# One-core delta-rule attention with two expert layers: two weight blocks loaded at a time from the first on, and eight stores of K Kᵀ moved from GpSimd's queue to SyncE's, behind 19 blocks

## The chip, the cores and the metric

One core of a Trainium2 chip runs the whole program. The time is device microseconds of that core, from launch to end; the number that is predicted is the median of repeated runs.

## What is computed

For each of 4 x 8 heads a state of 48 x 48 is carried over 768 tokens, and its 384 output features go through two expert layers. Cut to what matters:

```python
k_n = k / (norm(k) + 1e-6)
for t in range(S):
    y[:, :, t] = einsum('bhd,bhde->bhe', q[:, :, t], state)
    v_old = einsum('bhde,bhd->bhe', state, kt)
    state = state + bt * einsum('bhd,bhe->bhde', kt, vt - v_old)
x = y as (3072 tokens, 384)
h = max(x @ w_in, 0);  x = (h * h) @ w_out            # 384 -> 2048 -> 384
h = max(x @ w1, x @ w2, x @ w3);  out = h @ w_out2     # 384 -> 768 -> 384
```

## The kernel before

**Tiling.** The tokens are cut into 12 chunks of 64 (`c`), each chunk into two halves `p` of 16 heads. Inside a chunk the recurrence is solved in closed form: K Kᵀ of the chunk is turned into a triangular matrix whose inverse is built on DVE in blocks of 32 (`solve32`, lines 747 to 766). Chunks 0 and 1 are solved in a prologue, in blocks of 16 that PE joins afterwards (`join_z`, `join_w`, lines 952 to 971). Chunks 2 and 3 are solved later, from a K Kᵀ that is computed in the prologue too (`kk_matmul` with `second`, lines 939 to 949), copied by ACT into SBUF, stored to DRAM (`kk_d` the K Kᵀ part, `p_d` the Q Kᵀ part, eight stores of 256 KB) and read back in another layout by `start32` (line 315).

**Weights.** All weights are 64-bit floats in DRAM. A block of w_in (128 columns) or a row block of w_out is 384 KB; `fetch` (line 90) loads it on SyncE's queue, `turn` (line 116) makes two float32r parts of it. For each block ACT takes the sign away (line 107, for the first 12 blocks also line 112, else DVE's line 120), DVE joins the words (line 124), ACT rounds to the high part (line 128) and DVE subtracts to get the low part (line 132). There are 32 blocks: 0 to 11 are w_in into tiles `rawp`, then w_out and w_in take turns in seven buffers that are used in a ring (`raw` four, `big` three). So 19 blocks have a place of their own, and block 19 and on wait until a buffer is free.

**How many are under way.** Lines 97 to 99 give each of the first 19 blocks a wait: a block among the first 12 waits for the landing of the block ahead of it (`few = 1`), a later one for the landing of the second ahead (`few = 2`):

```python
few = 1 if len(raws) <= NP else 2
if few < len(raws) <= NP + NR + len(spare):
    tc.add_manual_dep(raws[-1], raws[-1 - few].name, ... reason="landed")
```

**Order.** The order on each engine is written in the program and pinned (`pin`, line 261). In `attention(0)` (line 1007) each step of chunk 0's attention is followed by the words of one or two blocks, so 12 blocks stand between the steps on ACT and DVE. After that `moe_a(0)` (line 581) is PE's main stream, with the remaining blocks (`weights`, line 775), the second join and chunk 1's attention between its steps; in the same way each later `moe_a(c)` carries the attention of chunk c + 1. From line 1066 on the second expert layer runs.

**Memory.** The prologue's tiles live in a pool `pkp` (`ks_more`, `kct`, `ksr`, `rawp`), which is closed at line 1016. The pools `gp` (`gh`, `gl`) and `moe` (`wout0` to `wout3`) take its place, so the first write of these waits until the old tiles are no longer read, by stores too.

**Queues.** SyncE issues keys and weight blocks in program order, and an instruction that waits holds up those behind it. GpSimd's queue issues the values and keys of attention (`load_att`, line 372), before also the eight stores (lines 946 and 948).

Of the kernel before, what the change touches and what calls it, by code (L numbers as in the profile page):

```python
# [36 lines left out]
U2 = 2 * Q  # L37


def delta_moe(ctx, tc, kc, ab, kt, vt, beta, beta32, beta16, kq, w_in, w_out, w1, w2, w3, w_out2, out):  # L40
    nc = tc.nc
    vec, act, pool = nc.vector, nc.scalar, nc.gpsimd
# [24 lines left out]
    kk_d = [dram.tile([2, C, 2, B * Q, C], F32, name=f"kk{g}", tag=f"kk{g}") for g in range(NC // 2)]  # L67
# [10 lines left out]
    NR, NP = 4, 12  # L78
# [11 lines left out]
    def fetch(src, shape, dma):  # L90
        raw = raw_tile(shape)
        names = "k n" if len(shape) == 2 else "n"
        flat = "k (n t)" if len(shape) == 2 else "(n t)"
        raws.append(dma.dma_start(raw.rearrange(f"p {names} t -> p {flat}"), src).ins)
        for i in raw_after:
            behind(raws[-1], i)
        few = 1 if len(raws) <= NP else 2
        if few < len(raws) <= NP + NR + len(spare):
            tc.add_manual_dep(raws[-1], raws[-1 - few].name, mybir.DependencyInfo(mybir.DependencyClass.Sync, mybir.DependencyReason.DATA), reason="landed")
        return raw  # L100

    def convert(src, hi, lo, shape, lo_eng, dma):
        turn(fetch(src, shape, dma), hi, lo, lo_eng)
# [60 lines left out]
    def two(d, c, p):  # L164

        return d[:, c, 2 * p:2 * p + 2]
# [9 lines left out]
    def kk_matmul(c, p, ps_, swap=1):  # L176

        k = kcs.pop((c, p))
        pk, pq = (ps_[0].tile([128, U2, C], F32, name=n, tag=ps_[1]) for n in ("pk", "pq"))
        for u in range(U2):  # L180
            for i, ps in enumerate((pk, pq)):
                for t in range(2):
                    r = slice(64 * t, 64 * t + D)
                    o = 64 * (t ^ i * swap)
                    pe.matmul(ps[o:o + 64, u], k[r, u, 0], k[r, u, i], start=True, stop=True)  # L185
        return pk, pq

    def kk_store(c, p, kk, dma=nc.sync):
        dma.dma_start(kk_d[c // 2].rearrange("t j c u i -> (t j) c u i")[:, c % 2, U2 * p:U2 * p + U2], kk)
# [71 lines left out]
    def pin():  # L261
        todo = []
        for i in reversed(nc.cur_bb.bb.instructions):
            if i.name == seen[0]:
                break
            todo.append(i)
        for i in reversed(todo):
            seen[0] = i.name
            if i.engine in pinned and i.name not in loose:
                if pinned[i.engine]:  # L270
                    behind(i, pinned[i.engine])
                pinned[i.engine] = i

    def behind(ins, before):

        tc.add_manual_dep(ins, before.name, mybir.DependencyInfo(mybir.DependencyClass.NoSync, mybir.DependencyReason.DATA), reason="order")
# [26 lines left out]
    def start32(g, dmas=(nc.sync, nc.sync)):  # L303
        cs = HALVED[g]
        u = 64 * len(cs)
        M = M32[0:u]
        a = early.tile([128, 32], F32, name="a32", tag="a32")[0:u]
        bt = early.tile([128, 32], F32, name="b32", tag="b32")[0:u]
        if g:
            dmas[0].dma_start(bt, beta_d[g].rearrange("x c u j -> (x c u) j"))  # L310
        else:
            halves[:] = [bt]
        for h, t, o in quarters if g else ():
            hs = slice(32 * h, 32 * h + 32)
            dmas[t].dma_start(M[o:o + 32], kk_d[g][t, hs, :, :, hs].rearrange("j c u i -> (c u) j i"))
        def ready():
            return prep(M, 32, u, bt, a, early, alone=not g, flip=g < 2)

        def norm(nm):
            pv = transposed(nm, 32, u).rearrange("j (s t c u) -> j c s t u", s=2, t=2, u=16)  # L320
            for t in range(2):
                for s in range(2):
                    o = 64 * t + 32 * s
                    i = act.activation(out=normT[o:o + 32, cs[0]:cs[0] + len(cs)], in_=pv[:, :, s, t], func=AF.Copy, scale=0.5)
            return i.ins
        return M, a, ready, norm
# [45 lines left out]
    def load_att(c, p):  # L372
        us = slice(U2 * p, U2 * p + U2)
        def load(to, src):
            pool.dma_start(to, src)
        kq_ = None
        if c:
            kq_ = att.tile([R2, U2, 2, C], F32, name="kq", tag="kq")
            i = pool.dma_start(kq_, two(kc, c, p).rearrange("p b q t s -> p (b q) t s"))
            for j in kq_after:  # L380
                behind(i.ins, j)
        v = att.tile([128, U2, D], F32, name="v", tag="v")
        load(v, two(vt, c, p).rearrange("p b q d -> p (b q) d"))
        pt_ = att.tile([128, U2, C], F32, name="p", tag="p")
        if c:
            pool.dma_start(pt_, p_d[c][:, us])
        kt_ = ktp[p]
        load(kt_[:, 0:U2 * D], two(kt, c, p).rearrange("p b q d -> p (b q d)"))
        tiles[c, p] = [kq_, v, xb[:, us], pt_, kt_, None, None, None, None]
# [336 lines left out]
    if True:  # L726
# [68 lines left out]
        for h in range(2):  # L795
            for n, (c, p) in enumerate(todo):
                i = (nc.sync, act)[p].dma_start(kcts[n][:, :, h], two(kc, c, p)[:, :, :, h].rearrange("p b q s -> p (b q) s"))
        M, a, _, norm = start32(0)
        bt = halves[0]
        for c in range(2):  # L800
# [6 lines left out]
        for n, dma in ((0, nc.sync), (1, act)):  # L807
            c, p = second[n]
            dma.dma_start(second_keys[n], two(kc, c, p).rearrange("p b q t s -> p (b q) t s"))
        wcols = lambda f: slice(128 * f, 128 * (f + 1))  # L810

        ins = lambda *fs: [(f, True) for f in fs]
# [95 lines left out]
        for n in range(2, 4):  # L908
            c, p = second[n]
# [20 lines left out]
            vec.tensor_tensor(out=of_, in0=of_, in1=tv, op=ALU.add)  # L930
        vec.memset(diagonal(M, 32), 1.0)
        vec.tensor_tensor(out=Mb, in0=Mb, in1=by_block(a, 2), op=ALU.mult)
        vec.transpose(out=turned_x.rearrange("p n i -> p i n"), in_=M)
        dt, zt = (wa.tile([128, KD, TB], F32R, name=n, tag=n, bufs=2).bitcast(F32).rearrange("p k t -> p (k t)")[:, 0:512].rearrange("p (n i) -> p n i", i=16) for n in ("xh", "xl"))
        last_turn = vec.transpose(out=dt.rearrange("p n i -> p i n"), in_=M[:, :, 0:16].rearrange("p j i -> p i j")).ins
        solved.append(last_turn)
        pin()

        second_ks = [(kss[2][:, 0], kss[3][:, 0]), (ks_more[:, 0], ks_more[:, 1]), (kss[0][:, 1], kss[2][:, 1]), (kss[3][:, 1], kss[0][:, 0])]
        for n in range(4):  # L940
            c, p = second[n]
            kcs[c, p] = second_keys[n]
            for i, (k, pk) in enumerate(zip(second_ks[n], kk_matmul(c, p, (p1, at)[n % 2], 0))):
                act.copy(k, pk)
                if i:
                    pool.dma_start(p_d[c][:, U2 * p:U2 * p + U2], k)
                else:
                    kk_store(c, p, k, pool)
            pin()
        joins = {}  # L950

        def join_z(c):
# [18 lines left out]
            return vec.tensor_sub(out=to, in0=to, in1=joins[c]).ins  # L971

        join_z(0)
        sign_next(1)
        joined = join_w(0)
        pin()
        pinned.clear()
# [196 lines left out]
```

## Time and profile before

| what | us |
|---|---|
| median of 3 runs | 942.15 (940.6 to 942.8) |
| profiled execution, its own time | 945.85 |
| its span in the trace | 944.1 |
| outside the span | 1.75 |
| mean granted clock of TensorE | 0.956 |

The rows further down are of the profiled execution. In a timeline row the first number is the start in us from the span's start, the second the time taken, then engine, line, operation, tiles; in brackets stands how long the engine had been idle and what ended that. "issue" there means that nothing in the profile ended the wait. A `q` behind an engine's name (SPq) is its queue, where DMAs are issued.

### The profile page before, as it was taken

The page shows a single profiled execution, that of the slowest core. Times are in us where ns is not written, and L with a number is a line of the kernel's source. Part 1 is how long each engine was busy: PE and PEld are TensorE (multiplying, and loading weights), DVE is VectorE, ACT ScalarE, POOL GpSimd, SP SyncE. Part 2 cuts the span into 40 slices and gives each one's busy share as a digit, 9 for nine tenths or more (in the row PEclk, how much of TensorE's full clock was granted, in tenths as well). Part 3 has the DMA queues.
Part 4 walks back from the last instruction along what each step waited for, and adds up shares of the span by engine and source line. Part 5 has one row for each costly group of instructions (what it writes and reads, how often), then busy time and mean ns, then how long its engine had stood idle before and what let it go on. Part 6 is the DMA issues. An engine that isn't in the chain of part 4 may idle for free.

```text
span 944.1 us, 27438 instructions
## 1 busy us (share of the span) xinstructions
PE 890.2 (94%) x11958; PEld 863.9 (92%) x11958; DVE 469.3 (50%) x1044; ACT 389.0 (41%) x824; POOL 141.4 (15%) x238
## 2 busy tenths in 40 slices
PE   7563899899999999999999999999999999999998
PEld 7553898799899999999999999999999999999998
DVE  5445778449726852784378354456332323323221
ACT  5454754335344534453444466565221222212211
POOL 6310210032222123112401320002000000000000
PEclk8765889799999999999999999999999999999999
DMA  9756723381475167326521743235201101000000
GB/s 239 225 163 198 216 88 92 98 182 41 113 219 123 64 143 184 99 64 178 135 73 63 169 140 87 65 104 142 60 19 41 34 26 34 18 26 9 17 17 34
DMA packets 113527, 95.43 MB, mean 101 GB/s; under 512 B 69880, under 2 KB 95240, under 8 KB 113408
## 3 DMA queue, kind: packets, MB, share of 16 engines
q1 hardware_dynamic: 93824, 52.84, 21.5%
q0 software_dynamic: 12352, 34.75, 13.1%
q10 hardware_dynamic: 7232, 6.10, 2.1%
q8 instruction: 94, 1.54, 0.7%
q14 instruction: 25, 0.20, 0.1%
HBM read 70.45 MB, written 22.77 MB: 99 GB/s over the span
## 4 chain that ended last, share of the span: by engine, by line
PE 79%; DMA 9%; DVE 7%; ACT 3%; issue 1%; DVEq 0%; SPq 0%
PE p L1082 24%; PE px L613 19%; PE p L593 19%; PE po L1099 8%; DMA rawp<-in_moe_w_in_dram 7%; DMA raw<-in_moe_w_out_dram 2%; PE pY L537 2%; PE pk L185 1%; PE pU L483 1%; DVE gl L602 1%; DVE buf L293 1%; PE pW L437 1%; DVE buf L294 1%; PE pA L464 1%; PE pq L185 1%
## 5 line engine op out<-in xcount | busy, mean ns | idle before, releaser
L1082 PE MATMUL p<-x_h,w 128*128 128x384 f32 x864 | 220.0, 336 | 0.0
L613 PE MATMUL px<-wout,gh 128*128 128x384 f32 x768 | 202.3, 344 | 0.0
L593 PE MATMUL p<-xh,win_h 128*128 128x256 f32 x576 | 171.8, 298 | 1.6 <-DVE gl L602 0.9
L593 PE MATMUL p<-xl,win_h 128*128 128x256 f32 x576 | 165.8, 288 | 0.3 <-DVE xl L559 0.3
L593 PE MATMUL p<-xh,win_l 128*128 128x256 f32 x576 | 165.9, 288 | 0.0
L1082 PEld LDWEIGHTS p<-x_h,w 128*128 128x128 f32 x864 | 156.2, 188 | 0.0
L1082 PE MATMUL p<-x_l,w 128*128 128x384 f32 x432 | 145.2, 336 | 0.0
L602 DVE TENSOR_TENSOR gl<-p,gh 128x512 fp32r<-128x512 f32 x96 | 66.3, 691 | 145.5 <-ACT gh L601 142.0
L613 PEld LDWEIGHTS px<-wout,gh 128*128 128x128 f32 x768 | 137.5, 192 | 1.2
L613 PE MATMUL px<-wout,gl 128*128 128x384 f32 x384 | 130.5, 340 | 0.0
L599 ACT ACTIVATE p<-p 128x512 f32<-128x512 f32 x96 | 55.9, 582 | 172.1 <-PE p L593 172.1
L593 PEld LDWEIGHTS p<-xh,win_h 128*128 128x128 f32 x576 | 112.6, 196 | 5.5 <-DVE gl L602 1.5
L593 PEld LDWEIGHTS p<-xl,win_h 128*128 128x128 f32 x576 | 113.1, 196 | 0.6 <-DVE xl L559 0.5
L593 PEld LDWEIGHTS p<-xh,win_l 128*128 128x128 f32 x576 | 113.0, 196 | 0.1
L1088 DVE TENSOR_TENSOR mx<-p,mx 128x384 f32<-128x384 f32 x48 | 26.8, 558 | 127.6 <-PE p L1082 127.3
L1082 PEld LDWEIGHTS p<-x_l,w 128*128 128x128 f32 x432 | 81.2, 188 | 0.0
L1090 ACT CAST hh<-mx 128x384 fp32r<-128x384 f32 x48 | 24.6, 513 | 126.2 <-DVE mx L1089 126.0
L613 PEld LDWEIGHTS px<-wout,gl 128*128 128x128 f32 x384 | 73.5, 191 | 0.0
L601 ACT CAST gh<-p 128x512 fp32r<-128x512 f32 x96 | 56.4, 587 | 2.6
L600 ACT ACTIVATE p<-p 128x512 f32<-128x512 f32 x96 | 56.0, 583 | 2.7
L294 DVE TENSOR_TENSOR buf<-buf 128x30 f32<-128x30 f32 (+9 forms) x150 | 49.8, 332 | 5.0
L293 DVE TENSOR_TENSOR buf<-buf 128x30 f32<-128x30 f32 (+9 forms) x150 | 49.4, 329 | 3.9
(190 smaller groups left out, 1345.2 us busy)
## 6 DMA issues: line engine op xcount, KB each, us to landing
kq<-in_kc_dram POOLq DMA_DIRECT2D x22, 448.0 KB, 5.2
raw<-in_moe_w_dram SPq DMA_DIRECT2D x18, 384.0 KB, 3.8
raw<-in_moe_w_out_dram SPq DMA_DIRECT2D x16, 384.0 KB, 4.1
p<-p POOLq DMA_DIRECT2D x22, 256.0 KB, 3.8
rawp<-in_moe_w_in_dram SPq DMA_DIRECT2D x12, 384.0 KB, 4.2
v<-in_vt_dram POOLq DMA_DIRECT2D x24, 192.0 KB, 3.0
ktp<-in_kt_dram POOLq DMA_DIRECT2D x24, 192.0 KB, 4.2
x<-xs SPq DMA_DIRECT2D x48, 96.0 KB, 3.2
```

Of the source, the lines that this page charges most:

```text
L293: eng.tensor_tensor(out=tv, in0=col.unsqueeze(2).broadcast_to([u, k, l]), in1=row.unsqueeze(1).broadcast_to([u, k, l]), op=ALU.mult)
L294: i = eng.tensor_tensor(out=of_, in0=of_, in1=tv, op=ALU.add)
L593: pe.matmul(p1[:, j], w[:, k, f], x[c][:, k], start=n == 0 and j == 0, stop=n == 8, skip_group_check=True)
L599: act.activation(out=p1, in_=p1, func=AF.Relu)
L600: act.activation(out=p1, in_=p1, func=AF.Square)
L601: last_gh[0] = act.copy(gh, p1).ins
L602: last_gl[0] = vec.tensor_sub(out=gl, in0=p1, in1=gh.bitcast(F32)).ins
L613: g = pe.matmul(px[:, h, 0:DM], x[:, j, hs], w, start=f == 0 and i == 0, stop=f == NF - 1 and i == 2, skip_group_check=True)
L1082: pe.matmul(p, w[i][:, k, fs], x[:, k], start=n == 0, stop=n == 8)
L1088: vec.tensor_max(out=t, in0=ps[1], in1=t)
L1090: act.copy(hh[:, f], t2)
L1099: pe.matmul(po[:, 0:DM], x[:, f, js], w[:, f], start=i == 0, stop=i == 17)
```

## The change

1. `fetch` gives each of the first 19 blocks a wait through a new function `landed`, which keeps one list of DMAs, `under_way`: each waits for the landing of the third last in the list, so two are under way. The loads of the first keys stand in the list ahead of the blocks (the last two of them count).
2. The eight stores of the second K Kᵀ go from GpSimd's queue to SyncE's, in program order behind block 18, and through `landed` as well: first the four of `kk_d`, then the four of `p_d`.
3. In `load_att(1, p)` on GpSimd the load of `kq` comes behind the load of `p`.
4. The turn of the solved matrix (line 933, one transpose of 128 x 1024) is made in two halves, columns 16 to 31 first, then the transpose that the second matmul of the join needs, then columns 0 to 15.
5. `sign_next(2)` in place of `sign_next(1)`: ACT's two sign steps of block 1 stand ahead of attention(0) with those of block 0.

```diff
-        few = 1 if len(raws) <= NP else 2
-        if few < len(raws) <= NP + NR + len(spare):
-            tc.add_manual_dep(raws[-1], raws[-1 - few].name, ...)
+        if len(raws) <= NP + NR + len(spare):
+            landed(raws[-1])
+    under_way = []
+    def landed(ins):
+        under_way.append(ins)
+        if len(under_way) > 2:
+            tc.add_manual_dep(ins, under_way[-3].name, ...)
...
                 i = (nc.sync, act)[p].dma_start(kcts[n][:, :, h], ...)
+                under_way.append(i.ins)
...
+        del under_way[:-2]
...
-        vec.transpose(out=turned_x.rearrange("p n i -> p i n"), in_=M)
+        turned_i = turned_x.rearrange("p n i -> p i n")
+        vec.transpose(out=turned_i[:, 16:32], in_=M[:, 16:32])
         last_turn = vec.transpose(out=dt..., in_=M[:, :, 0:16]...).ins
+        vec.transpose(out=turned_i[:, 0:16], in_=M[:, 0:16])
...
                 act.copy(k, pk)
-                if i:
-                    pool.dma_start(p_d[c][:, U2 * p:U2 * p + U2], k)
-                else:
-                    kk_store(c, p, k, pool)
+        for i in range(2):
+            for (c, p), ks in zip(second, second_ks):
+                to = p_d[c][:, us] if i else kk_d[c // 2]...
+                landed(nc.sync.dma_start(to, ks[i]).ins)
...
-        sign_next(1)
+        sign_next(2)
```

What this does to the order of instructions is seen at three places. In these rows a name's number is that of the tile; lines below are those of the kernel they come from (line 94 keeps its number, 189 and 946 became 961, 315 became 322, 128 became 135).

SyncE, before, from the last of the first 19 blocks (row 1) to the first blocks that wait for a free buffer; what a row waits for stands in brackets (DMAHW is the landing of another DMA of SyncE's or ACT's queue):

```order
L94 DMA big_132<-in_moe_w_in_dram 128x3x256 [waits DMAHW2_49]
L94 DMA raw_1050<-in_moe_w_in_dram 128x3x256 [waits DVE_49]
L94 DMA raw_1057<-in_moe_w_out_dram 128x768 [waits DVE_49]
L94 DMA raw_1165<-in_moe_w_out_dram 128x768 [waits DVE_49]
L94 DMA raw_1172<-in_moe_w_in_dram 128x3x256 [waits DVE_49]
```

SyncE at the same place, after:

```order
L94 DMA big_132<-in_moe_w_in_dram 128x3x256 [waits DMAHW2_49]
L961 DMA kk1_94<-ksr0_161 128x512 [waits DMAHW3_49,Activation_49]
L961 DMA kk1_94<-ks_more_141 128x512 [waits DMAHW4_49,DVE_49,Activation_49]
L961 DMA kk1_94<-buf_133 128x512 [waits DMAHW5_49,Activation_49]
L961 DMA p2_101<-ksr1_162 128x512 [waits DMAHW7_49]
L961 DMA kk1_94<-ksr1_162 128x512 [waits DMAHW6_49,Activation_49]
L961 DMA p3_102<-ksr0_161 128x512 [waits DMAHW0_49]
L961 DMA p2_101<-ks_more_141 128x512 [waits DMAHW1_49]
L961 DMA p3_102<-buf_133 128x512 [waits DMAHW3_49,Activation_49]
L94 DMA raw_1051<-in_moe_w_in_dram 128x3x256 [waits DVE_49]
```

Eight stores now stand between block 18 and block 19. The first two wait for blocks 17 and 18, the third for the first, the fourth in the row (`p2<-ksr1`) for the third, the sixth for the fourth, the last for the seventh.

ACT, before, where the first block of w_out is rounded into `wout0` (DMASW is a landing of GpSimd's queue, there the old stores from `ksr`):

```order
L107 ACTIVATE raw_209<-raw_209 128x384 [waits DMAHW6_49]
L128 CAST win_h_130<-rawp11_207 128x3x128 [waits DVE_49]
L107 ACTIVATE raw_211<-raw_211 128x384 [waits DMAHW7_49]
L128 CAST wout0_1044<-raw_209 128x384 [waits DMASW6_49,DMASW5_49,DMASW7_49,DMASW4_49,DVE_49]
L107 ACTIVATE raw_213<-raw_213 128x384 [waits DMAHW0_49]
```

ACT there, after:

```order
L114 ACTIVATE raw_209<-raw_209 128x384 [waits DMAHW6_49]
L135 CAST win_h_130<-rawp11_207 128x3x128 [waits DVE_49]
L114 ACTIVATE raw_211<-raw_211 128x384 [waits DMAHW7_49]
L135 CAST wout0_1045<-raw_209 128x384 [waits DMAHW2_49,DMAHW1_49,DMAHW5_49,DMAHW0_49,DVE_49]
L114 ACTIVATE raw_213<-raw_213 128x384
```

The order is the same; the rounding into `wout0` waits for four stores of SyncE's queue instead of four of GpSimd's: all those that read `ksr`, of which `p3<-ksr0` is issued last.

GpSimd, before, from the last store of chunk 1's scores on (`kk1` is K Kᵀ of chunks 2 and 3, `k21`, `v`, `p`, `kq` and `ktp` belong to chunk 1's attention):

```order
L379 DMA kq_1013<-in_kc_dram 112x1024
L189 DMA kk1_94<-ksr0_161 128x512
L946 DMA p2_101<-ksr1_162 128x512
L379 DMA kq_1020<-in_kc_dram 112x1024
...
L315 DMA buf_133<-kk1_94 32x32x32 x4
L347 DMA k21_1393<-kk0_93 32x16x32 x2
L375 DMA v_1015<-in_vt_dram 128x384
L375 DMA v_1022<-in_vt_dram 128x384
L386 DMA p_1017<-p1_100 128x512
L386 DMA p_1024<-p1_100 128x512
```

GpSimd there, after:

```order
L322 DMA buf_133<-kk1_94 32x32x32 x4
L354 DMA k21_1394<-kk0_93 32x16x32 x2
L382 DMA v_1016<-in_vt_dram 128x384
L382 DMA v_1023<-in_vt_dram 128x384
L391 DMA p_1018<-p1_100 128x512
L386 DMA kq_1014<-in_kc_dram 112x1024
L391 DMA p_1025<-p1_100 128x512
L386 DMA kq_1021<-in_kc_dram 112x1024
```

The stores are gone, the read-back of K Kᵀ (which needs the four `kk1` stores landed) is the next thing in the queue, and chunk 1's keys `kq` come behind it.

## Rows read from the trace of the kernel before

**Rows 1.** Busy time by engine in four stretches; last columns granted clock, DMA share, GB/s.

```profile
0.00:85.00 85.00, 48.69 (x1154) 44.70 (x1154) 39.43 (x95) 39.72 (x94) 26.71 (x55) 0.70 0.76 210
85.00:130.00 45.00, 39.37 (x684) 37.84 (x685) 35.24 (x86) 31.05 (x65) 6.52 (x9) 0.80 0.56 164
130.00:300.00 170.00, 163.77 (x2882) 155.56 (x2880) 100.85 (x236) 74.78 (x160) 35.29 (x58) 0.96 0.47 121
300.00:940.00 640.00, 637.72 (x7240) 625.46 (x7240) 293.75 (x630) 242.98 (x506) 72.83 (x116) 1.00 0.29 77
```

**Rows 2.** The chain that ended last, in order of time: start, us, what.

```profile
6.29 14.04 DMA rawp<-in_moe_w_in_dram
20.35 4.29 DMA rawp<-in_moe_w_in_dram
24.66 7.36 DMA rawp<-in_moe_w_in_dram
...
61.71 3.13 DMA rawp<-in_moe_w_in_dram
...
75.71 3.57 DMA raw<-in_moe_w_out_dram
```

**Rows 3.** DVE around its longest wait; then its waits, 60 to 80 us (total, times, longest).

```profile
60.92 0.55 DVE L559 TENSOR_TENSOR xl<-pT,xh 128x384 fp32r<-128x384 f32 x1
...
79.31 0.36 DVE L120 TENSOR_SCALAR raw<-raw 128x384 int32<-128x384 int32 x1 [1.71 <-DMA raw<-in_moe_w_out_dram]
...
DVE raw L120 <- DMA raw<-in_moe_w_out_dram: 16.7, 4, 12.0
```

**Rows 4.** Timeline of PE at the first join, and where it waits for DVE.

```profile
29.46 0.79 PE L962 MATMUL pZ<-buf,big 32*32 32x16 f32 x66
34.74 1.04 PE L962 MATMUL pZ<-buf,big 32*32 32x16 f32 x62 [4.49 <-issue]
...
68.43 0.41 PE L593 MATMUL p<-xl,win_h 128*128 128x256 f32 x1
81.59 1.10 PE L959 MATMUL pW<-ident 32*32 32x128 f32 x16 [12.75 <-DVE Sb L524]
```

**Rows 5.** Timeline of SyncE's issues with two blocks under way, to block 19.

```profile
75.71 0.33 SPq L94 DMA_DIRECT2D raw<-in_moe_w_out_dram  x1
...
80.75 0.38 SPq L94 DMA_DIRECT2D big<-in_moe_w_in_dram  x1
...
86.25 0.38 SPq L94 DMA_DIRECT2D raw<-in_moe_w_in_dram  x1
```

**Rows 6.** Timeline of ACT: block 7's sign, xh, first w_out rounding, block 19's sign.

```profile
58.51 0.54 ACT L107 ACTIVATE rawp<-rawp 128x384 f32<-128x384 f32 x1 [2.70 <-DMA rawp<-in_moe_w_in_dram]
58.96 0.52 ACT L112 ACTIVATE rawp<-rawp 128x384 int32<-128x384 uint16 x1
59.38 0.46 ACT L558 CAST xh<-pT 128x384 fp32r<-128x384 f32 x1
84.38 0.54 ACT L128 CAST wout<-raw 128x384 fp32r<-128x384 f32 x1 [0.42 <-DVE raw L124]
93.35 0.56 ACT L107 ACTIVATE raw<-raw 128x384 f32<-128x384 f32 x1
```

**Rows 7.** Stores of K Kᵀ: issue, KB each, median us to landing; then all of line 189.

```profile
kk<-buf SPq DMA_DIRECT2D x8, 256.0 KB, 4.3
kk<-ksr POOLq DMA_DIRECT2D x2, 256.0 KB, 7.1
DMA to landing us min/median/max: 3.0/4.7/8.8
```

**Rows 8.** Busy time in one stretch with a single block under way, as rows 1.

```profile
60.00:62.00 2.00, 1.41 (x26) 1.41 (x28) 1.47 (x4) 1.41 (x4) 0.00 (x0) 0.50 0.51 176
```

**Rows 9.** Timeline of DVE at the turn of the solved matrix.

```profile
26.10 1.98 DVE L933 STREAM_TRANSPOSE buf<-buf 128x1024 f32<-128x1024 f32 x1
```

**Rows 10.** Timeline of GpSimd: the last of its loads for chunk 1.

```profile
65.44 0.54 POOL L375 DMA_DIRECT2D ktp<-in_kt_dram  x1 [2.06 <-PE pD L515]
```

More of the change, by code (lines that the diff above doesn't have):

```diff
@@ L96, in fetch @@
             behind(raws[-1], i)
-        few = 1 if len(raws) <= NP else 2
-        if few < len(raws) <= NP + NR + len(spare):
-            tc.add_manual_dep(raws[-1], raws[-1 - few].name, mybir.DependencyInfo(mybir.DependencyClass.Sync, mybir.DependencyReason.DATA), reason="landed")
-        return raw
+        if len(raws) <= NP + NR + len(spare):
+            landed(raws[-1])
+        return raw
+    under_way = []
+    def landed(ins):
+        under_way.append(ins)
+        if len(under_way) > 2:
+            tc.add_manual_dep(ins, under_way[-3].name, mybir.DependencyInfo(mybir.DependencyClass.Sync, mybir.DependencyReason.DATA), reason="landed")
     def convert(src, hi, lo, shape, lo_eng, dma):
@@ L378, in load_att @@
             kq_ = att.tile([R2, U2, 2, C], F32, name="kq", tag="kq")
-            i = pool.dma_start(kq_, two(kc, c, p).rearrange("p b q t s -> p (b q) t s"))
-            for j in kq_after:
-                behind(i.ins, j)
+            i_kq = pool.dma_start(kq_, two(kc, c, p).rearrange("p b q t s -> p (b q) t s")).ins
         v = att.tile([128, U2, D], F32, name="v", tag="v")
@@ L385, in load_att @@
         if c:
-            pool.dma_start(pt_, p_d[c][:, us])
+            i = pool.dma_start(pt_, p_d[c][:, us])
+            if c == 1:
+                behind(i_kq, i.ins)
         kt_ = ktp[p]
@@ L942, in delta_moe @@
             kcs[c, p] = second_keys[n]
-            for i, (k, pk) in enumerate(zip(second_ks[n], kk_matmul(c, p, (p1, at)[n % 2], 0))):
+            for k, pk in zip(second_ks[n], kk_matmul(c, p, (p1, at)[n % 2], 0)):
                 act.copy(k, pk)
-                if i:
-                    pool.dma_start(p_d[c][:, U2 * p:U2 * p + U2], k)
-                else:
-                    kk_store(c, p, k, pool)
             pin()
+        for i in range(2):
+            for (c, p), ks in zip(second, second_ks):
+                us = slice(U2 * p, U2 * p + U2)
+                to = p_d[c][:, us] if i else kk_d[c // 2].rearrange("t j c u i -> (t j) c u i")[:, c % 2, us]
+                landed(nc.sync.dma_start(to, ks[i]).ins)
         joins = {}
```

## The prediction

> **What bounds the kernel now.** I read the busy table by stretch first. From 130 us on PE is all but full, 163.77 of 170 us and 637.72 of 640 us; in the first 85 us it is busy for 48.69 us only [rows 1]. What can be won is won in the first 130 us, and what shifts there shifts the end, because the order of work on every engine behind it stays as it is. Next I read the chain of waits in that stretch: from 6.29 us to 79.28 us it is one load of a weight block after the other, with nothing else between [rows 2]. The single blocks are the thing to see. With DMA quiet a block lands 3.13 us after its issue; the first three, beside other loads, take 14.04, 4.29 and 7.36 us. And while one block is under way the DMA engines are half idle: share 0.51 at 176 GB/s [rows 8]. So the chain is latency, one block at a time, and not bandwidth.
>
> Then who waits for it. DVE finishes the last `xl` of chunk 0 at 61.5 us and stands until 79.31 us in front of four line-120 steps for blocks 12 to 15, four waits of 16.7 us in all, the longest 12.0 us, the last 1.71 us [rows 3]. Behind them, in DVE's order, is the copy of the state that frees PE's accumulator: PE waits 12.75 us for it [rows 4]. ACT waits 2.70 us for block 7 in front of `xh` [rows 6]. That is the stall of the prologue.
>
> **The change part by part.** The sum is made in the profiled execution and measured at one place: the first rounding into `wout0`, which ACT starts at 84.38 us [rows 6].
>
> Two blocks under way. The trace has this already for blocks 12 to 18: with two under way blocks 15 and 18 are issued at 75.71 and 80.75 us with blocks 16 and 17 between [rows 5], 5.04 us for three, 1.68 us a block. I take 1.75 us for w_in blocks too, whose rows are shorter; the bounds are 1.14 us (384 KB at the full rate that 176 GB/s at share 0.51 gives, 345 GB/s) and 3.13 us (nothing won from the second) [rows 2, 8]. Block 0 now waits for the keys, so it starts some 4 us after 6.29 us; I take its landing as before, 20.3 us, since before it queued behind the keys and the second keys on the same queue. From there 17 blocks at 1.75 us give 50 us, and 1.5 us more for the crowded stretch up to 24 us: block 17 lands at about 51.5 us (bounds 47 and 57), block 15 at 48 us instead of 79.3 us. DVE's four waits go. What is late next is ACT's signing of blocks 8 to 11, eight steps at about 0.45 us (58.51 to 58.96 us [rows 6]) from ACT's last `xh` on; I find them ready within 0.3 us of when DVE asks. Gain 16.5 us.
>
> Block 7 is there in time too, at some 34 us, so `xh` starts when PE's transposes are done instead of behind the 2.70 us wait. Gain 2.7 us, in front of the 16.5 us, so they add.
>
> PE stands 4.49 us in the middle of the 128 matmuls of line 962, with nothing in the profile that releases it [rows 4]. I read this as a fetch of instructions behind a full DMA: the stores and keys of GpSimd's queue run just then, and they leave. Bounds: nothing, and the whole 4.49 us; I take 2.5 us, near the middle, since two weight blocks remain under way there. The Trainium skill, "Runtime: NRT & Kernel Launch", section "Instruction fetch mechanics", says that crossing a block of instructions costs one tail bump that is mostly hidden. The 4.49 us without a releaser speaks against that here; by the page the 2.5 us would be no gain and the sum 15.0 us.
>
> `sign_next(2)` takes two ACT steps of 0.45 us out of attention(0), between the two matmul groups of the first chunk, and puts them where ACT waits for the join. Gain 1.0 us (0 to 1.3). The turn in two halves: DVE's whole turn ends at 28.08 us and PE reaches the join's second matmul group at 29.46 us [rows 4, 9], so PE is the late one; PE's own chain hides this edit, and were it not there it would be worth 1.0 us, half of 1.98 us. No gain. The order of `kq` and `p` on GpSimd: nobody asks for either before chunk 1's attention; nothing.
>
> Together 16.5 + 2.7 + 2.5 + 1.0 = 22.7 us: ACT would ask for `wout0` at 61.7 us.
>
> The new wait. `wout0` lies where `ksr` lay, and the rounding now waits for the stores of `ksr` on SyncE, the sixth of eight (`p3<-ksr0`). Four stores follow one another to there: the first waits for block 17, the third store for the first, the fourth for the third, the sixth for the fourth. A store of that size on SyncE took 3.0 us at the least and 4.3 us in the median; on GpSimd, all at once, 7.1 us [rows 7]. I take 3.5 us, near the least, since at most two are under way: 14.0 us, and 0.5 us for the read-back of K Kᵀ that starts beside the last. 51.5 + 14.5 = 66.0 us, so ACT waits 4.3 us (bounds: no wait, with 3.0 us a store from 49 us; 10.6 us, with 4.7 us from 53 us). What is queued behind it on ACT is all of the remaining rounding and the first layer's activations, and DVE and PE wait for these, so this comes off in full. The Trainium skill, "DMA: Bandwidth & Descriptors", section "Anatomy of one DMA — SWDGE (gpsimd) path", has a DMA cost 2.0 us plus bytes at 436 GB/s: an estimate of 2.6 us a store and 2.9 us a block. By that the stores would be through before ACT asks and the gain would be 21.8 us. The lone block's 3.13 us and the store's least 3.0 us lie 0.2 to 0.4 us above the page, so it is short here.
>
> Blocks 19 and on. On SyncE they are now behind the eight stores. Their buffers come free when `wout0` has been rounded, so block 19 was issued 1.9 us after ACT's start there (86.25 us) and ACT asked for it at 93.35 us [rows 5, 6]; by 68 us the last store is issued, so the queue holds nothing up. But GpSimd's loads for chunk 1, the last of which was issued at 65.44 us [rows 10], now start behind the read-back, at about 65 us, and meet blocks 19 to 22. ACT has 7.1 us for block 19; beside such loads blocks took 4.29 to 7.36 us [rows 2]. I take 0.9 us off (0 to 7).
>
> Net: 22.7 - 4.3 - 0.9 = 17.5 us. The profiled execution took 945.85 us with 944.1 us of span, so it would take 928.35 us. It stands 3.7 us above the median of the runs; the forecast goes by the median: 942.15 - 17.5 = 924.65 us.
>
> **The rivals.** *A, the shift is partly eaten between 62 and 110 us.* The change moves some 2.1 MB of stores and 2.2 MB of chunk 1's loads into the stretch in which blocks 19 to 31 come through, and DVE is busy there for 35.24 of 45 us [rows 1]. 4.3 MB are 12.5 us of full DMA at 345 GB/s. For it: that stretch waits for blocks too. Against it: DMA was at 0.56 there, 20 us of slack in 45 us [rows 1]. If half of it lands in front of a block, 6 us go, and with stores at their slower bound another 4 us: gain 7 us, 935 us.
>
> *B, two blocks under way bring little, and the stores decide: slower.* If two blocks share what one had, at 3.5 us a block [rows 2], block 17 lands at 82 us as before, the four stores make it 96 us, and ACT's 84.38 us becomes 96 us: 942.15 + 12 = 954 us. It turns from gain to loss where block 17 lands later than 70 us. Against it are the issues at 1.68 us in rows 5, in the same trace and of the same size. What remains is that w_in rows are shorter, and the crowd up to 24 us.
>
> *C, it does not do what it says:* PE would be late at the same place anyway, by its own first matmuls of the layer. These 18 were over at 68.84 us, in the shadow of the wait for DVE [rows 4], at the lower of the two levels of granted clock (0.50 [rows 8]). Moved ahead by the 6.2 us that the chunk's attention gains they end near 62.6 us, about when ACT and DVE get there, so they cost at most 1 us. About no change, 942 us, would need that the wait for DVE [rows 4] is not the true one.
>
> *D, more:* no store wait, and PE's whole 4.49 us: about 917 us.
>
> **How the numbers follow.** Forecast, 918 to 931 us: 0.72, 924.65 us. A, 931 to 940 us: 0.14. B, slower: 0.06. C, no change: 0.04. D: 0.04. The range that should hold the time eight times in ten runs from 917 us (D) to 934 us (slower stores, the better part of A). A measurement of this kernel tells about 0.2%, 1.9 us, from no change. Faster by more: 0.72 + 0.14 + 0.04 = 0.90; within: 0.04; slower: 0.06.
>
> **What would show it.** Right: SyncE issues blocks 2 to 18 about 1.75 us apart, block 15 lands near 48 us, DVE has no wait at line 120 for blocks 12 to 15, and PE's 12.75 us wait [rows 4] is gone; ACT waits some 4 us at the first rounding into `wout0`, with a DMA of `ksr` as the releaser, near 66 us; PE's stop inside line 962 is about 2 us. Wrong: blocks 3 us apart with two under way (B); a wait for block 19 or later that was not there (A); ACT's wait for the stores 10 us or more; or the gain at 85 us is there but PE's idle time between 100 and 300 us has grown, which would mean that what follows was not shifted as a whole.

## The result: 10.2 us faster, where 17.5 us were forecast

The changed kernel takes 932.25 us in the median (930.45 to 934.91, 4 runs), the kernel before took 942.47 us beside it (940.6 to 942.9, 4 runs): a ratio of 0.9898, 95% interval 0.987 to 0.9925. On the chip of a later group of experiments it was 930.51 us (930.05 to 933.25) against 943.55 us, 0.9868 (0.9841 to 0.9895). The profiled execution took 934.91 us with a span of 933.2 us, 10.9 us less than before. The median lies within the 917 to 934 us of the prediction, but outside the 918 to 931 us of its forecast and among the 931 to 940 us that it gave to rival A.

The busy table of after, in the columns of [rows 1] (span of the stretch, then PE, PEld, DVE, ACT, POOL, granted clock, DMA share, GB/s):

```profile
0.00:85.00 85.00, 62.54 (x1461) 58.08 (x1462) 50.38 (x121) 50.02 (x117) 23.44 (x49) 0.70 0.83 225
85.00:130.00 45.00, 37.53 (x620) 35.49 (x619) 29.90 (x74) 27.55 (x61) 8.73 (x14) 0.92 0.59 167
130.00:300.00 170.00, 163.76 (x2926) 155.56 (x2926) 105.56 (x250) 73.84 (x154) 33.16 (x54) 0.96 0.49 121
300.00:930.00 630.00, 626.67 (x6979) 614.59 (x6964) 284.16 (x602) 236.73 (x493) 71.52 (x114) 1.00 0.29 76
```

As forecast, the gain is in the first stretch (PE 62.54 us busy against 48.69 us), and 130 to 300 us is as full as it was. The timelines of PE, DVE and ACT in after show the waits of [rows 3, 4, 6] going, and the new one:

```profile
30.80 0.79 PE L974 MATMUL pZ<-buf,big 32*32 32x16 f32 x66
32.07 0.70 PE L974 MATMUL pZ<-buf,big 32*32 32x16 f32 x62 [0.48 <-issue]
...
53.64 0.46 ACT L565 CAST xh<-pT 128x384 fp32r<-128x384 f32 x1
...
55.65 1.16 DVE L127 TENSOR_SCALAR raw<-raw 128x384 int32<-128x384 int32 x4
...
63.03 0.85 PE L971 MATMUL pW<-ident 32*32 32x128 f32 x16
...
66.42 0.54 ACT L135 CAST wout<-raw 128x384 fp32r<-128x384 f32 x1 [4.75 <-DMA p<-ksr]
```

PE's 4.49 us stop is down to 0.48 us, `xh` starts with no wait, DVE's four sign steps run back to back, and the matmuls of the second join that PE had waited 12.75 us for start at 63.03 us without a wait, where it was 81.59 us [rows 4]. ACT asks for `wout0` at 61.67 us and waits 4.75 us for a store.

SyncE's queue in after: blocks 1 and 2, blocks 15 and 18, then stores and block 19.

```profile
13.09 0.39 SPq L94 DMA_DIRECT2D rawp<-in_moe_w_in_dram  x1
20.76 0.37 SPq L94 DMA_DIRECT2D rawp<-in_moe_w_in_dram  x1
...
48.68 0.33 SPq L94 DMA_DIRECT2D raw<-in_moe_w_out_dram  x1
54.38 0.38 SPq L94 DMA_DIRECT2D big<-in_moe_w_in_dram  x1
56.12 0.33 SPq L961 DMA_DIRECT2D kk<-ksr  x1
58.04 0.33 SPq L961 DMA_DIRECT2D kk<-ks_more  x1
58.76 0.32 SPq L961 DMA_DIRECT2D kk<-buf  x1
62.11 0.32 SPq L961 DMA_DIRECT2D p<-ksr  x1
...
64.17 0.32 SPq L961 DMA_DIRECT2D p<-ksr  x1
...
69.18 0.43 SPq L94 DMA_DIRECT2D raw<-in_moe_w_in_dram  x1
```

Where the lead over the kernel before was won, and where it went again:

| place | before | after | lead |
|---|---|---|---|
| second half of the join's first matmuls, PE | 34.74 | 32.07 | 2.67 |
| first of the last two `xh` of chunk 0, ACT | 59.38 | 53.64 | 5.74 |
| first rounding into `wout0`, ACT | 84.38 | 66.42 | 17.96 |
| first w matmuls of chunk 1's attention (line 437, after 444), PE | 126.34 | 114.59 | 11.75 |
| end of the span | 944.1 | 933.2 | 10.9 |

So 6.2 us are lost between 66 and 115 us. The chain of waits of after says to what (start, us, what):

```profile
70.24 11.41 DMA raw<-in_moe_w_out_dram
...
83.80 10.81 DMA big<-in_moe_w_out_dram
...
99.63 5.91 DMA big<-in_moe_w_out_dram
...
114.59 1.20 PE pW L444 x63
```

Two blocks take 11 us each, where [rows 2] had 3.13 us for one alone. Beside them, GpSimd's timeline of after: the read-back of K Kᵀ starts only when the stores are down, and chunk 1's loads follow it, up to 76.68 us. The last row is the busy table's, for 75 to 80 us: the DMA engines are full, with a share of 1.03 (a packet is counted whole in the stretch in which it starts, so that a share can pass 1).

```profile
65.61 3.14 POOL L322 DMA_DIRECT2D buf<-kk  x4 [43.68 <-DMA kk<-ksr]
...
71.67 0.54 POOL L386 DMA_DIRECT2D kq<-in_kc_dram  x1
...
76.68 0.54 POOL L382 DMA_DIRECT2D ktp<-in_kt_dram  x1 [1.02 <-DMA k<-kk]
```

```profile
75.00:80.00 5.00, 2.53 (x134) 2.49 (x135) 1.30 (x3) 2.45 (x5) 1.09 (x2) 0.50 1.03 333
```

Over all of blocks 19 to 31 that is seen in the time from a block's issue to its landing, as far as the trace gives it; first the kernel before, then after:

```profile
DMA to landing us min/median/max: 3.3/4.8/6.1
DMA to landing us min/median/max: 4.4/10.3/16.8
```

### The profile page after: what moved, and what is told of

Its sections match the earlier page's. It is cut to its first block, busy times and chain, and to the rows that moved or that the text cites. A ratio compares the mean times of both kernels' runs of the same rounds, so it can differ in the third digit from the quotient of the medians.

```text
span 933.2 us, 27437 instructions
## 1 busy us (share of the span) xinstructions
PE 890.5 (95%) x11958; PEld 863.7 (93%) x11958; DVE 470.0 (50%) x1045; ACT 388.4 (42%) x824; POOL 136.9 (15%) x230
## 4 chain that ended last, share of the span: by engine, by line
PE 77%; DMA 10%; DVE 7%; ACT 3%; issue 1%; POOL 0%; ACTq 0%; SPq 0%; DVEq 0%; POOLq 0%
PE p L1094 24%; PE px L620 18%; PE p L600 18%; PE po L1111 8%; DMA rawp<-in_moe_w_in_dram 3%; DMA big<-in_moe_w_out_dram 2%; PE pY L544 2%; DMA raw<-in_moe_w_out_dram 2%; PE pk L192 1%; PE pU L490 1%; DMA kct<-in_kc_dram 1%; DVE gl L609 1%; DVE buf L300 1%; DMA xb<-xt 1%; DVE buf L301 1%
```

## Experiments on the prologue

Theory: the gain comes from two blocks under way, and the 6.2 us go because GpSimd's read-back and chunk 1's loads now run beside blocks 19 and on. Rivals: the moved stores themselves are the gain; or the 6.2 us are not a collision but what conversion can't do faster.

**Blocks two at a time, stores left on GpSimd's queue.**

```diff
-        for i in range(2):
-            for (c, p), ks in zip(second, second_ks):
-                ...
-                landed(nc.sync.dma_start(to, ks[i]).ins)
...
+                if i:
+                    pool.dma_start(p_d[c][:, U2 * p:U2 * p + U2], k)
+                else:
+                    kk_store(c, p, k, pool)
```

> The changed kernel, but the eight stores of the second K K^T stay on GpSimd's queue where they were before the change; the blocks go two at a time. In the changed kernel the first rounding into wout0 moved from 84.4 to 66.4 us, but the end moved by 10.9 us only. Theory (collision): the loss of some 6 us between 66 and 115 us comes from chunk 1's loads on GpSimd's queue, which since the change start behind the read-back at 65.6 us and meet blocks 19 to 25. Here these loads are issued by some 60 us as before the change, so blocks 19 to 25 land 3 to 6 us after their issue, the rounding into wout0 has no store to wait for, and the stretch from it to the end is as long as before the change: block 15 near 53 us, that rounding at 62 to 66 us, 921 to 927 us. Rival (the stores had to leave): the stores take the DMA from the first blocks, which come 3.5 us apart up to 40 us, block 15 lands after 60 us, and the time is 932 us or more.

932.75 us (929.5 to 938.29, 6 runs), ratio 0.9882 (0.9848 to 0.9916): no different from the full change, so the end did not come out at the theory's 921 to 927 us, but where the rival had it, at 932 us or more. The stretch did: from the first rounding into `wout0` to chunk 1's w it takes 42.77 us, against 48.17 us in after and 41.96 us before. But that rounding starts later. Its chain, and under it ACT's timeline:

```profile
56.05 7.72 DMA big<-in_moe_w_out_dram
...
111.34 1.20 PE pW L444 x63
```

```profile
68.57 0.55 ACT L135 CAST wout<-raw 128x384 fp32r<-128x384 f32 x1 [0.45 <-DVE raw L131]
```

Chunk 1's loads now run from 49 to 63 us and meet blocks 14 to 17 instead; one of them takes 7.72 us of the chain. The collision moved. It is not all of the delay: as the rival had it, the stores take part of the DMA from the first blocks too. From 25 to 45 us its engines are full,

```profile
25.00:45.00 20.00, 11.36 (x539) 10.63 (x536) 8.01 (x16) 8.76 (x17) 6.37 (x11) 0.75 0.99 296
```

and blocks 2 to 11 are issued 2.9 us apart, where it is 2.3 us in after, so that block 11 goes out 4.1 us later (45.58 against 41.44 us).

**Stores moved, blocks one at a time as before.**

```diff
-        if len(raws) <= NP + NR + len(spare):
-            landed(raws[-1])
+        few = 1 if len(raws) <= NP else 2
+        if few < len(raws) <= NP + NR + len(spare):
+            tc.add_manual_dep(raws[-1], raws[-1 - few].name, ...)
+        under_way.append(raws[-1])
```

> The changed kernel, but the first 12 blocks go one at a time as before the change; the stores are on SyncE's queue behind block 18. Collision theory: without the stores and the keys beside them blocks 2 to 11 come 3.2 to 3.5 us apart instead of 4 to 7, block 17 lands near 70 us, four stores of 2.6 us each put the rounding into wout0 at 80 us, 4 us earlier than before the change, and chunk 1's loads then cost 4 to 6 us again: 940 to 946 us, no gain worth the name. Rival from the prediction (one block at a time lands block 17 at 82 us as before): rounding at 93 us or later, 950 us or more.

944.47 us (942.66 to 949.13, 10 runs), ratio 1.0012 (0.9989 to 1.0036). Blocks come 3.2 to 3.9 us apart, block 17 lands at 70.9 us, and ACT's wait for the stores grows to what the other waits were:

```profile
81.05 0.53 ACT L137 CAST wout<-raw 128x384 fp32r<-128x384 f32 x1 [9.36 <-DMA p<-ksr]
```

The time lies in the 940 to 946 us that the theory gave. So moving the stores alone is worth nothing; the whole gain needs two blocks under way.

**The read-back behind chunk 1's loads on GpSimd's queue**, all else as changed.

```diff
-            dmas[t].dma_start(M[o:o + 32], kk_d[g][t, ...])
+            i = dmas[t].dma_start(M[o:o + 32], kk_d[g][t, ...])
+            if g == 1:
+                behind(i.ins, kt_load[0])
```

> The changed kernel, with one edge more on GpSimd's queue: the read-back of K K^T (which waits for the stores until 65.6 us) comes behind chunk 1's loads v, p, kq, ktp instead of ahead of them; so these go out by 62 us, beside blocks 8 to 17. Collision theory: the rounding into wout0 stays at 66 to 68 us, blocks 20 to 25 land 4 to 7 us after their issue instead of 11 to 14, and 4 to 6 us come back: 926 to 929 us. Rival (the words of blocks 19 to 31 on ACT and DVE, or block 19's late issue behind the last store, take the time, not the loads beside them): 931 to 934 us as the changed kernel.

936.13 us (931.31 to 938.45, 6 runs), ratio 0.9907 (0.9873 to 0.994): a miss. Again the stretch is short, 43.47 us, so that the loads are the cause there; again they do the harm earlier. Block 17, issued at 52.11 us, lands at 62.19 us, the stores come after it, and ACT waits 10.80 us for them. The read-back now runs beside block 19 in place of the loads, and the stretch is short all the same.

**The four stores that read `ksr` first**, each behind the one ahead in the queue.

```diff
-        for i in range(2):
-            for (c, p), ks in zip(second, second_ks):
+        for n, i in ((0, 0), (3, 0), (0, 1), (2, 1), (1, 0), (1, 1), (2, 0), (3, 1)):
+            for (c, p), ks in ((second[n], second_ks[n]),):
...
+                landed(stored[-1])
+                if len(stored) > 1:
+                    behind(stored[-1], stored[-2])
```

> The changed kernel with the eight stores in another order on SyncE, the four that read ksr first, so that the rounding into wout0 waits for the fourth store in place of the sixth. Both theories: ACT's wait of 4.75 us there falls to 0 to 1.5 us. Collision theory: blocks 19 on are still issued behind the last store at 69 us and come at the pace of a full DMA, so at most 2 us of it reach the end: 930 to 933 us. Rival (ACT and DVE words are the bound behind 66 us): all of the 4 us reach the end: 927 to 929 us.

934.86 us (928.71 to 935.84, 6 runs), ratio 0.9884 (0.9849 to 0.9919), above what either theory expected. ACT's wait falls to 1.66 us and `wout0` starts at 63.85 us, 2.6 us ahead of after. Nothing is left of it: GpSimd's loads are later still (to 80.1 us), blocks 19 to 31 take 15.4 us in the median from issue to landing, up to 21.2 us, and one of them holds the chain for longer than any block of after:

```profile
82.71 16.38 DMA raw<-in_moe_w_out_dram
```

With two under way each placement tried costs some block or store about as much as another saves. But with the stores moved DMA is not full ahead of them: 0.66 from 25 to 45 us. So the next theory was that the number under way still holds the stream.

**Three under way, in place of two; the changed kernel beside it.**

```diff
-        if len(under_way) > 2:
-            tc.add_manual_dep(ins, under_way[-3].name, ...)
+        if len(under_way) > 3:
+            tc.add_manual_dep(ins, under_way[-4].name, ...)
...
-        del under_way[:-2]
+        del under_way[:-3]
```

> The changed kernel with three loads or stores under way instead of two, among blocks and stores alike; nothing else. If the number under way is what holds the stream of blocks (DMA busy for 0.61 to 0.77 only between 25 and 62 us with two), blocks 2 to 18 come about 1.7 us apart instead of 2.1, block 17 lands near 49 us instead of 56.1, the four stores in a chain end before ACT asks for the first rounding of w_out, and the whole is 926 to 929 us against 932. If what holds it is what DMA can move in all, or each transfer is slower by as much as there are more of them, block 17 still lands at 55 to 57 us and the time is 931 to 934 us. If three transfers disturb the first keys or GpSimd's read-back, PE's stop in the join is back at 3 us or more and the time is 934 to 938 us.

> The changed kernel itself on the same chip as the three others, as their base: 932.25 us, within 1.5 us, by every theory.

930.1 us (923.42 to 933.5, 6 runs), ratio 0.9848 (0.9812 to 0.9883); the changed kernel beside it 930.51 us, 0.9868 (0.9841 to 0.9895). In time that is undecided, between what the two theories expected. In the trace the first one holds: the busy table from 25 to 45 us, after and then with three under way,

```profile
25.00:45.00 20.00, 14.02 (x588) 13.02 (x586) 9.24 (x16) 10.92 (x22) 0.00 (x0) 0.76 0.66 193
```

```profile
25.00:45.00 20.00, 11.67 (x548) 10.94 (x546) 7.54 (x13) 8.74 (x17) 0.00 (x0) 0.76 0.86 283
```

In the run with the stores moved and blocks one at a time the same stretch has

```profile
25.00:45.00 20.00, 14.76 (x604) 13.88 (x600) 10.72 (x19) 12.83 (x27) 0.00 (x0) 0.73 0.40 123
```

With one, two and three under way DMA moves 123, 193 and 283 GB/s. With three the store that waits for block 17 is issued at 49.11 us, and ACT's wait for the stores is over (timelines of that run):

```profile
49.11 0.33 SPq L961 DMA_DIRECT2D kk<-ks_more  x1
...
64.84 0.55 ACT L135 CAST wout<-raw 128x384 fp32r<-128x384 f32 x1 [0.16 <-DVE raw L131]
...
65.70 1.08 POOL L382 DMA_DIRECT2D ktp<-in_kt_dram  x2
...
66.70 0.38 SPq L94 DMA_DIRECT2D raw<-in_moe_w_in_dram  x1
```

Now chunk 1's loads are all issued before block 19 is, and chunk 1's w, at 108.55 us, stands 6.0 us ahead of after.

**Three under way, stores on GpSimd's queue** (the first experiment and the last one together).

> As the run with blocks two at a time and the stores left on GpSimd's queue (932.75 us), but three under way. By the theory of too few under way: w_out's first rounding at 64 to 66 us instead of 68.57, and 927 to 930 us. By the rival, that all DMA together is the bound: blocks 15 to 17 beside GpSimd's loads at 60 to 63 us take longer than the 7.72 us that block 16 took, and the time stays at 931 to 935 us.

929.33 us (924.24 to 932.96, 6 runs), ratio 0.9845 (0.9813 to 0.9877), within the 927 to 930 us that the theory gave; w of chunk 1 at 106.25 us. With three under way it makes no difference that can be measured on which queue the stores are.

All fourteen profiled executions side by side show where the 6.2 us went. The stretch is that from the first rounding into `wout0` to chunk 1's w; all in us.

| kernel | last chunk 1 load issued | block 19 issued | load behind block | stretch |
|---|---|---|---|---|
| before | 65.4 | 86.3 | -20.8 | 41.96 |
| loads ahead of read-back | 60.5 | 74.4 | -13.9 | 43.47 |
| blocks only | 62.6 | 70.4 | -7.8 | 42.77 |
| three, stores on GpSimd | 62.2 | 65.9 | -3.7 | 42.22 |
| the same, z later (below) | 64.0 | 67.7 | -3.7 | 42.64 |
| three | 66.2 | 66.7 | -0.5 | 43.71 |
| three, z later still (below) | 64.7 | 65.1 | -0.4 | 44.10 |
| three, z later (below) | 66.1 | 65.9 | 0.2 | 44.27 |
| stores only | 89.6 | 82.2 | 7.4 | 45.87 |
| after | 76.7 | 69.2 | 7.5 | 48.17 |
| after, z later (below) | 76.3 | 68.4 | 7.8 | 47.41 |
| after, again | 76.3 | 68.2 | 8.1 | 47.24 |
| turn and sign undone (below) | 77.1 | 66.1 | 11.0 | 48.09 |
| `ksr` stores first | 80.1 | 66.6 | 13.5 | 53.10 |

Where the last load is issued before block 19 or within 0.2 us behind it the stretch is 42.0 to 44.3 us, where it comes 7.4 us or more behind it 45.9 to 53.1 us, and the longest belongs to the latest loads. The conversion of blocks 19 to 31, the rival, is the same work in all of them, and the run with the read-back moved differs from after in nothing but the order on GpSimd's queue. Nor is it that blocks 19 to 22 are issued closer together: they take 3.20 us in the run with the turn and the sign undone (66.12 to 69.32 us) and 3.25 us before (86.25 to 89.50 us), and the stretch is 48.09 us in one and 41.96 us in the other.

**The turn in one, and block 1's signs back in the first chunk's attention.**

```diff
-        vec.transpose(out=turned_i[:, 16:32], in_=M[:, 16:32])
+        vec.transpose(out=turned_x.rearrange("p n i -> p i n"), in_=M)
...
-        vec.transpose(out=turned_i[:, 0:16], in_=M[:, 0:16])
...
-        sign_next(2)
+        sign_next(1)
```

> The changed kernel with two parts undone: the solved matrix is turned in one transpose, and block 1's two sign steps come back into the first chunk's attention. By the prediction's sum the turn is worth nothing and the sign steps 1.0 us (0 to 1.3), so 932 to 934 us. Rival: both are hidden, since ACT's wait for the stores takes up any time won ahead of it, and the time is within 0.5 us of the changed kernel's. Second rival: PE is no longer late at the join and the turn costs its half, 1.0 us more: 934 to 935 us.

934.02 us (930.53 to 935.38, 6 runs), ratio 0.9889 (0.9863 to 0.9916): 3.5 us above the changed kernel beside it, with intervals that overlap. The trace shows no cost: `wout0` starts at 64.97 us and chunk 1's w at 113.06 us, both ahead of after. What these two parts are worth stays open.

## Experiments behind the prologue

The leads at chunk 1's w did not all reach the end. The two profiled executions of the changed kernel itself stand at 114.59 and 114.30 us there, and their spans are 933.2 and 928.8 us. The busy table in steps of 5 us shows most of that: once between 130 and 300 us, near 160 us (175 us before), the granted clock is at the lower of its two levels while PE is full. After:

```profile
155.00:160.00 5.00, 4.59 (x38) 4.20 (x32) 3.33 (x9) 2.34 (x4) 0.00 (x0) 1.00 0.70 200
160.00:165.00 5.00, 2.41 (x66) 2.35 (x67) 3.02 (x4) 2.23 (x4) 0.00 (x0) 0.75 0.02 4
165.00:170.00 5.00, 5.00 (x79) 4.66 (x79) 0.69 (x1) 0.79 (x2) 0.00 (x0) 0.50 0.09 14
170.00:175.00 5.00, 5.00 (x76) 4.71 (x75) 1.29 (x2) 2.90 (x5) 1.33 (x2) 0.50 0.65 197
175.00:180.00 5.00, 5.00 (x123) 4.56 (x126) 1.57 (x4) 0.87 (x3) 2.13 (x4) 0.89 0.22 60
```

A row of 5 us with a mean clock c was at the lower level for 5 x 2 x (1 - c): 2.5 + 5 + 5 + 1.1 = 13.6 us in all. If PE works at half its rate there, as its clock does, it cost half of that, an estimate of 6.8 us. The same kernel in its other profiled execution has 6.9 us of it: by the same estimate 3.4 us cheaper, by chance. Of the first ten profiles five had some 13.6 us and five 6.8 to 6.9 us. In all ten PE stops for 3.00 us there, and the fall begins within 1 us of the end of that stop, in after here:

```profile
162.59 1.99 PE L434 MATMUL pZ<-xb,k 32*32 32x32 f32 x64 [3.00 <-ACT xb L368]
```

That is the start of chunk 2's attention, which waits for DVE's turn of the solved matrix and ACT's copies of it. It has nothing to do with the change, and its cure is another place in PE's order: z and w of chunk 2 two steps later.

```diff
-                extra += [..., ([13, 19, 20, 22, 24, 27, 30], attention(2))]
+                extra += [..., ([13, 19, 22, 24, 25, 28, 30], attention(2))]
```

> The changed kernel, with one thing moved far behind the change: the z and w matmuls of chunk 2's attention (lines 434 and 444) come two steps later in PE's order (steps 22 and 24 in place of 20 and 22, the next two at 25 and 28). In every profile so far PE stops for exactly 3.00 us there, and the granted clock falls from 1.00 to 0.50 right behind that stop, for 6.8 us in some executions and 13.6 us in others, with PE busy throughout. If the stop brings the fall, both go: 3.0 us and 3.4 or 6.8 us, so 921 to 926 us, and the spread of the runs becomes smaller, since the two lengths are gone. If the fall comes from something else (the place in time, the sort of work), only the 3.0 us go: 927.5 to 929.5 us. If the work only stops a little later instead, for the w matmuls, 930 to 932 us as before.

930.45 us (926.77 to 932.19, 6 runs), ratio 0.986 (0.9829 to 0.989): not the 921 to 926 us of the theory, but the 930 to 932 us expected for a stop that only moves. The stop had shrunk and got another releaser:

```profile
163.54 1.94 PE L434 MATMUL pZ<-xb,k 32*32 32x32 f32 x64 [1.57 <-ACT buf L208]
```

PE now waits for an accumulator that ACT has yet to read, behind its three copies, and the clock still falls, for 6.8 us in this run. Then the same edit with three under way.

> Three loads or stores under way and chunk 2's z two steps later. The two places are 50 us apart, so by the theory the gains add: what three under way win in the stream of blocks (the first w matmul of chunk 1 at 108.6 instead of 114.3 us in the profiles) and what the stop at 160 us costs: 916 to 922 us. If three under way win nothing at the end, as their time so far (930.1 against 930.5 us) allows, it comes out with the run with two under way.

926.14 us (923.89 to 929.2, 6 runs), ratio 0.9817 (0.979 to 0.9845): 4.3 us below the run with two under way beside it, and short of the 916 to 922 us expected, with the 1.57 us stop and the fall still there, for 3.4 us. The intervals overlap by little, 0.9829 to 0.9845, so three under way do seem to win at the end; with the 3.00 us stop in place no gain of theirs showed above the scatter.

The stores on GpSimd's queue, three under way, z later:

> Three under way among the blocks, the stores left on GpSimd's queue, and chunk 2's z two steps later. By the theory, 915 to 921 us, a little below the run with the stores moved, since the first w matmul of chunk 1 stood at 106.3 us here against 108.6 us. If moving the stores is worth something by itself, it is the slower of the two by 1 us or more.

926.34 us (924.52 to 930.29, 6 runs), ratio 0.9825 (0.9796 to 0.9854), not the 915 to 921 us expected: again no difference between the queues of the stores.

Then z two steps later still, with w right behind: `[13, 19, 24, 25, 27, 29, 30]`, and three under way.

> Three loads or stores under way, and chunk 2's z at step 24 with w right behind it at 25 (before: 22 and 24). With z at step 22 PE still stopped for 1.57 us, now for a buffer that ACT had not read yet, and the clock still fell to 0.50 behind it, for 3.4 us. By the theory that a stop of PE brings the fall: no stop over 0.5 us at line 434, no fall of the clock between 140 and 200 us, and 1.6 + 1.7 = 3.3 us less, 922 to 924.5 us against 926.14. If the fall comes without a stop, it is still there for 3.4 us or more, and the time is 924.5 to 926 us. If PE stops for w or for the last transposes of chunk 2 in place of z, 926 to 928 us.

922.82 us (921.69 to 926.68, 6 runs), ratio 0.9787 (0.9759 to 0.9815), as expected. PE's timeline and the busy table at that place:

```profile
157.71 1.20 PE L434 MATMUL pZ<-xb,k 32*32 32x32 f32 x64
...
160.41 1.20 PE L444 MATMUL pW<-k,xT 32*32 32x32 f32 x64 [0.23 <-DVE xT L427]
```

```profile
155.00:160.00 5.00, 5.00 (x91) 4.68 (x90) 1.85 (x4) 4.39 (x8) 0.00 (x0) 1.00 0.72 197
160.00:165.00 5.00, 3.77 (x139) 3.38 (x138) 0.95 (x2) 1.74 (x3) 1.33 (x2) 1.00 0.13 32
165.00:170.00 5.00, 5.00 (x85) 4.52 (x83) 2.77 (x6) 2.62 (x6) 2.43 (x4) 1.00 0.90 247
```

The stop is gone and so is the fall: 1.00 from 125 to 300 us. This is the fastest version, 20.3 us below the kernel before. One profile without the stop and without a fall at this place, against thirteen with both, is what this rests on. That a stop brings a fall is made likely by it and not more: what decides whether a stop does was not tested.

## Why the prediction held, and why its gain was 7 us too large

- **What bounds it, and the four waits of DVE.** Right. One block at a time was the bound; the stores alone gave nothing, 944.47 us. ACT asked for `wout0` at 61.67 us, forecast 61.7 us; ahead of `xh` 5.7 us were won and not 6.2 us, behind it 17.0 us and not 16.5 us.
- **The pitch of the blocks.** Mis-sized. Blocks 2 to 18 were issued in 33.6 us, 2.10 us apart and not 1.75 us, and block 17 landed at 56.1 us and not 51.5 us, still within the 47 to 57 us. The 1.75 us came from three issues in [rows 5], mostly of w_out. In after blocks 2 to 11, all w_in, come 2.3 us apart and blocks 12 to 18, mostly w_out, 2.0 us, so the shorter rows of w_in can be a part of it only.
- **The stores.** Mis-sized the other way. The chain of four took 2.64, 3.35, 2.06 and 2.08 us, 10.1 us together and not 14.0 us. The Trainium skill, "DMA: Bandwidth & Descriptors", section "Anatomy of one DMA — SWDGE (gpsimd) path", has 2.0 us plus bytes at 436 GB/s for DMAs that GpSimd issues; carried over to these stores of SyncE that is an estimate of 2.6 us each. The trace agrees with that better than with the 3.5 us taken from [rows 7]. The two errors, 4.6 us and 3.9 us, hide each other by luck: the rounding started at 66.42 us, forecast 66.0 us, and ACT's wait was 4.75 us, forecast 4.3 us.
- **PE's stop.** It went from 4.49 to 0.48 us, 4.0 us and not 2.5 us. PE reached the place 1.3 us later, so the lead behind it was 2.7 us. In the second profile of the same kernel the stop is 1.27 us. That it is a fetch of instructions, which the prediction only read into it, the traces bear out: they have 94 instruction packets of 16 KB, and in all thirteen profiles with a stop at this place PE goes on 1.2 to 1.6 us after one of them has ended (before: packet to 33.31 us, PE at 34.74 us; after: 30.68 and 32.07 us). The length of PE's stop goes with how full DMA is from 27 to 34 us: there is no stop at a share of 0.40 (stores moved, blocks one at a time), it is 0.48 us at 0.60 (after), 1.82 us at 0.88 (three under way), 2.64 to 2.92 us at 1.00 to 1.05 (stores on GpSimd's queue, two or three blocks under way), and it was 4.49 us at 1.03 before. The Trainium skill, "Runtime: NRT & Kernel Launch", section "Instruction fetch mechanics", has the cost of crossing a block of instructions as mostly hidden. The trace agrees for most of the kernel and not here: of the 94 packets before, four are followed so by a stop of over 0.7 us, the longest of them this one of 4.49 us.
- **Blocks 19 and on.** Mis-sized, and this term makes most of the miss. The prediction saw that chunk 1's loads would meet blocks 19 to 22, and priced that at 0.9 us (0 to 7) from blocks of 4.29 to 7.36 us beside other loads. Two that the chain waits for took 11.41 and 10.81 us, and 6.2 us were lost, 5.3 us more than priced. The other 2 us of the 7.3 us are 0.4 us at the first rounding, 0.9 us behind chunk 1's w, and the 0.7 us by which the profiled pair differs from the medians. The last store was issued at 68.82 us and not by 68 us, so block 19, at 69.18 us, was held up a little as well. It is rival A's mechanism, and about the 6 us that it worked out for the stretch from its DMA load; the chance of it was held at 0.14, with an average DMA share of 0.56 as the reason. From 75 to 80 us the share was 1.03. A's slower stores, its other 4 us, did not come, which fits a time at the lower end of its range.
- **The small parts.** The turn was forecast at nothing and the signs at 1.0 us; the run without both doesn't decide.
- **Rivals B and C.** Two under way don't share what one had (B): 193 GB/s against 123 GB/s. And the wait for DVE was the true one (C). Where the blocks do stay some 3.5 us apart, B's price was too high: it put block 17 at 82 us and ACT's start at 96 us, and the run with the stores alone had them at 70.9 and 81.05 us.
- **The rest of the lead**, 11.75 us at chunk 1's w, reached the end but for 0.9 us. The warning sign for it, more idle time of PE from 100 to 300 us, did come: PE is busy there for 187.81 us against 189.83 us, 2.0 us more idle. All of that lies ahead of 130 us, in the stretch that waits for blocks; from there to 300 us it is 163.76 us against 163.77 us.

## What to carry to other kernels

When a change brings transfers forward, list what else becomes ready at the same moment and price each block that meets them by the worst row of a crowd (here [rows 2] had one of 14.04 us), not by the mean DMA share of the stretch. Moving one batch of loads out of another's way helps only if DMA has idle time at the new place; here that was made by one more load under way, not by a better order. And look for a short stop of PE in a full stretch: where the clock falls behind it, it costs more than its own length.

## What the runs showed of the hardware

- A block of 384 KB that takes 3.13 us alone took 4.4 to 16.8 us, 10.3 us in the median, beside GpSimd's loads (blocks 19 to 31 of after), and up to 21.2 us in the run with the `ksr` stores first.
- With one, two and three loads under way DMA moved 123, 193 and 283 GB/s in the same stretch, 25 to 45 us, at shares of 0.40, 0.66 and 0.86.
- PE's stops without a releaser at the first join ended 1.2 to 1.6 us after a 16 KB instruction packet, in thirteen of thirteen profiles, and were 0.48 us long at a DMA share of 0.60 and 2.64 to 4.49 us at 1.00 to 1.05; at 0.40 there was none.
- PE's granted clock fell to its lower level, 1.2 of 2.4 GHz, during or right behind a single stop of 3.00 or 1.57 us in a full stretch, and stayed there for 13.6, 6.8 or 3.4 us with PE busy for nearly all of it. How long it lasted differed between executions of one kernel, an estimated 3.4 us of scatter in the time. The length of the stop alone does not tell whether it falls: behind stops of 1.42 us (near 229 us in after) and 0.99 us (near 163 us in the last run) it did not, while near 430 us it fell for 3.4 us behind one of 1.24 us (the run with the loads ahead of the read-back), and in the two runs with three under way and z two steps later behind 1.66 and 1.77 us.
